# Second layer of a two-layer MLP in fp32 on one core: seven half-size products, before by rounds of four, after as four column streams

## Chip, cores and metric

The kernel runs on one core of a Trainium2 chip. The metric is the device time in microseconds (us) of that core. Three runs of the kernel before gave 2251.70, 2251.74 and 2251.78 us; the median is 2251.74 us.

## What is computed

The input x has 8 sequences of 4096 tokens with 192 channels. A causal convolution with 7 taps (weights by a softmax over the taps, one set for each of 8 heads) gives y. Then comes an MLP on the 32768 tokens with 2048 hidden channels:

```
h = y @ w_in                              # 192 -> 2048
g = h * clip(h + 3.0, 0.0, 6.0) / 6.0
out = g @ w_out                           # 2048 -> 192
```

## The kernel before

The tokens are worked in 32 blocks of 1024 (NB = 32, TB = 1024). A block is two groups of N = 512 tokens. Block 0 goes another way (out_direct) and is not touched, apart from the work that is put beside it. Each of the blocks 1 to 31 runs first_layer (L477) and then second_layer (L532). The loop over the blocks stands at the end of the kernel, and `tc.manual_schedule()` means that every engine's instructions run in the order in which the code emits them.

**First layer.** The weights and y are each split into three parts (HIGH, LOW, MIX) and multiplied with f32r matmuls (L490): 16 steps of 18 matmuls of 512 columns, two at a time on the two halves of the rows. One group of tokens lies on the low partitions and the other on the high ones, so each part of y is also needed with its halves exchanged (`swap`, two DMAs on SP's queue, L265 and L266). ACT scales the partial sums (L501) and makes the clipped factor (relu, L301); DVE multiplies (gate, L305). Between the steps DVE does the convolution of the block after next, one tap at a time (L729). The result g has four quarters A11, A12, A21, A22 (token half by hidden half), each 128 partitions by 8 chunks by 512 tokens.

**Second layer.** The product of the 2 by 2 quarters of g with the 2 by 2 quarters of w_out is done by Strassen's scheme in Winograd's form: seven products instead of eight, with sums S1 to S4 of quarters of g and T1 to T4 of quarters of w_out (table `prod`, L405). S1 = A21 + A22 is added into A21 by a DMA that accumulates, issued by POOL (L528), and S3 = A11 - A21 is made on POOL (g_sums, L401), pair of chunks by pair, at the end of the first layer. S2 = S1 - A11 (into A11) and S4 = A12 - S2 (into A12) are made on DVE by the same helper, four chunks at a time.

A product has 96 output rows, which are three column strips of 32 (q = 0, 1, 2), and 8 chunks of 128 to contract. One matmul (L340) fills one strip of 32 columns of TensorE, so four run at once, in four strips (`tile_position`, `side_by_side` L347). The trace shows each fp32 matmul as two records, which are called passes here. Before, the 7 x 3 x 8 = 168 matmuls of a block go in rounds of four: `three` and `four` pack three strips of one product with one strip of another, and `by_quarters` splits the one strip left over by chunks. That makes 42 rounds, or 84 passes of four. The products are copied (L437, L540) or added (L445) from PSUM into SBUF tiles c0 to c4, transposed (L451) and stored (L359) by ACT, DVE and SP.

Around it stand `high_of` on ACT (L463), the LOW part (L742) and the MIX part (L466) on DVE, and their six exchanging DMAs, all emitted between the first and the second layer by halves_of_y; and conv[0], ACT's first tap (L727), inside the second layer. `left` is the end of a block, which runs inside the next block's first layer.

Of the kernel before, what the change touches and what calls it, by code (L numbers as in the profile page):

```python
# [25 lines left out]
def kernel(  # L26
# [90 lines left out]
    w_out = cst.tile([P, NP, 7, DH], F32, name="w_out")  # L117
    B11, B12, B21, B22, T1, T2, T4 = range(7)
    T3 = B12

    w_in_bits = moe_w_in.bitcast(U32).rearrange("(p s) (c f w) -> c p s f w", s=K3, f=P, w=2)
    w_out_bits = moe_w_out.bitcast(U32).rearrange("(k c p) w -> p c k w", p=P, k=2)
# [268 lines left out]
    def g_sums(engine, which, slots, width):  # L391

        forms = {
            3: (S3, A11, A21, ALU.subtract),
            2: (S2, S1, A11, ALU.subtract), 4: (S4, A12, S2, ALU.subtract),
        }
        for n in which:
            o, a, b, op = forms[n]
            for p in slots[::width]:
                r = slice(p, p + width)  # L400
                engine.tensor_tensor(out=o[:, r], in0=a[:, r], in1=b[:, r], op=op)  # L401


    prod = {
        1: (A11, B11), 2: (A12, B21), 3: (S4, B22), 4: (A22, T4),  # L405
        5: (S1, T1), 6: (S2, T2), 7: (None, T3),
    }

# [11 lines left out]
    def three(n, n4, q4):  # L420
        return four(*[(n, q) for q in range(NQ)], (n4, q4))
# [14 lines left out]
    def piece(dst, q, src, j):  # L436
        nc.scalar.copy(out=dst[rows(q)], in_=src[rows(j)])  # L437
# [21 lines left out]
    def r32(ap):  # L459
        return ap.bitcast(F32R)  # L460
# [13 lines left out]
        nc.scalar.mul(r32(mix), mix, -4096.0)  # L474

    free_slots = list(range(4))

    def first_layer(i, jobs):

        slots = {}  # L480

        def both(n):
            return psum[:, 2 * slots[n] : 2 * slots[n] + 2]

        def mms(n, part, start=False, stop=False):
            group, c = divmod(n, NP)
            for s in range(K3):
                for k in range(2):
                    r = slice(k * D2, (k + 1) * D2)
                    nc.tensor.matmul(  # L490
                        out=psum[:, 2 * slots[n] + k], lhsT=r32(w_in_parts[part][r, c, s]),
                        rhs=r32(y_parts[part][r, group, s]),
                        start=start and s == 0, stop=stop and s == K3 - 1,
                        skip_group_check=True,
                    )

        def begin(n):
            slots[n] = free_slots.pop(0)
            mms(n, HIGH, start=True)
            mms(n, LOW)  # L500
            nc.scalar.mul(both(n), both(n), 4097.0)  # L501

        def end(n):
            group, c = divmod(n, NP)
            mms(n, MIX, stop=True)
            to = g4[:, c, 1:3] if group else g4[:, c, 0::3]
            relu(to, both(n))
            gate(to, both(n))
            free_slots.append(slots[n])

        count = 2 * NP
        begin(0)
        begin(1)
        for job in jobs.get(-1, ()):
            job()
        for n in range(count):
            if n == count - 3:
                begin(n + 2)
            end(n)
            if n < count - 3:  # L520
                begin(n + 2)
            for job in jobs.get(n, ()):
                job()
            if n > NP and n % 2:
                pair = slice(n - NP - 1, n - NP + 1)
                g_sums(nc.gpsimd, (3,), range(NP)[pair], 2)
                if n + 1 < count:
                    nc.gpsimd.dma_start(out=S1[:, pair], in_=A22[:, pair], accum_op=ALU.add)  # L528
                else:
                    add(S1[:, pair], A21[:, pair], A22[:, pair])  # L530

    def second_layer(i, between):  # L532
        last = i + 1 == NB
        ours = [free_slots.pop(0) for _ in range(3 + last)]
        free_banks[:] = [2 * n + k for n in ours for k in range(2)]
        both = nc.sync, nc.scalar
        p1, p2, p4, u2, u3 = (cs.tile([DH, N], F32, name=f"c{k}") for k in range(5))
        two, third = rows_of(0, 2), rows_of(2, 3)
        b, bank = three(1, 2, 0)
        nc.scalar.copy(out=p1[:], in_=bank[m])  # L540
        piece(p2, 0, bank, NQ)
        b, bank = four((2, 1), (2, 2), (4, 0), (4, 1))
        for dst, q, j in ((p2, 1, 0), (p2, 2, 1), (p4, 0, 2), (p4, 1, 3)):
            piece(dst, q, bank, j)
        g_sums(nc.vector, (2,), every, 4)
        add(p2[:], p1[:], p2[:])
        store(i, p2, 0, 0)
        p5 = cs.tile([DH, N], F32, name="c1")
        b7, bank7 = three(7, 4, 2)
        piece(p4, 2, bank7, NQ)  # L550
        g_sums(nc.vector, (4,), every, 4)
        b, bank = three(6, 5, 0)
        piece(p5, 0, bank, NQ)
        add(u2[:], p1[:], bank[m])
        add(u3[:], u2[:], bank7[m])
        add(p4[:], u3[:], p4[:], ALU.subtract)
        store(i, p4, 1, 0)
        for job in between:
            job()
        b, bank = by_quarters(5, 1)  # L560
        pieces(p5, 1, bank)
        add(u2[two], u2[two], p5[two])
        add(p5[two], u3[two], p5[two])
        store(i, p5, 1, 1, range(2))

        def finish(bank, **part):
            t = part.get("tokens", slice(0, N))
            add(u2[:, t], u2[:, t], bank[m, t])
            add(u2[third, t], u2[third, t], bank[rows(NQ), t])
            store(i, u2, 0, 1, **part)  # L570
            add(u3[third, t], u3[third, t], bank[rows(NQ), t])
            store(i, u3, 1, 1, range(2, 3), **part)

        if last:
            for t in range(0, N, N // 2):
                bank = psum[:, take()]
                ts = slice(t, t + N // 2)
                side_by_side(*[
                    product(bank, j, n, q, tokens=ts)
                    for j, (n, q) in enumerate([(3, 0), (3, 1), (3, 2), (5, 2)])  # L580
                ])
                finish(bank, queues=both, tokens=ts)
            return []
        b, bank = three(3, 5, 2)
        free_slots.extend(ours)
        return [lambda: finish(bank)]

    def rows_of(q0, q1):
        return slice(q0 * QS, q1 * QS)
# [18 lines left out]
    with tc.manual_schedule():  # L608
# [106 lines left out]
        while n < len(units):  # L715
# [1 line left out]
            clamp(n + 1)  # L717
            split(n + 2)
            n += 1
        w_sums(((T1, B12, B11), (T2, B22, T1), (T4, T2, B21)))  # L720
        start_pools.close()
        late = ctx.enter_context(tc.tile_pool(name="late", bufs=1, reuse_waits="tile"))
        w_in_parts = [late.tile([P, NP, K3, P], F32, name=f"w_in{n}") for n in range(3)]
# [8 lines left out]
                ))  # L732
            return jobs

        y_parts = []

        def y_high():
            high_of(y_parts[HIGH][:, 0], y[:])
            swap(y_parts[HIGH][:, 1], y_parts[HIGH][:, 0])

        def y_low():
            nc.vector.tensor_tensor(  # L742
                out=r32(y_parts[LOW][:, 0]), in0=y[:], in1=y_parts[HIGH][:, 0], op=ALU.subtract
            )
            swap(y_parts[LOW][:, 1], y_parts[LOW][:, 0])

        def y_mix():
            from_high(y_parts[MIX][:, 0], y_parts[HIGH][:, 0], 1.0 + EPS, y[:], ALU.subtract)
            swap(y_parts[MIX][:, 1], y_parts[MIX][:, 0])

        def halves_of_y():
            y_high()
            y_low()
            y_mix()

        def prepare():
            for n in range(0, NP, 4):
                r = slice(n, n + 4)
                w_parts(*[w[:, r] for w in w_in_parts], w_in[:, r])
            for job in conv_jobs(1):  # L760
                job()
            first_in.close()
            later = ctx.enter_context(tc.tile_pool(name="later", bufs=1, reuse_waits="tile"))
            y_parts.extend(later.tile([P, 2, K3, N], F32, name=f"y{n}") for n in range(3))
            halves_of_y()
            x_tiles[2] = load_x(2, nc.gpsimd)

        out_direct(0, [prepare])
        w_sums(((T3, B22, B12),))
        last = ctx.enter_context(tc.tile_pool(name="last", bufs=1, reuse_waits="tile"))  # L770
        S3 = last.tile([P, NP, N], F32, name="s3")[:]
        cs = ctx.enter_context(tc.tile_pool(name="cs", bufs=1, reuse_waits="tile"))
# [2 lines left out]
        for i in range(1, NB):  # L775
            jobs = {2 * n + 1: [job] for n, job in enumerate(conv[1:])}
            jobs[-1] = left
            if i == 1:
                jobs = {n + 2: job for n, job in jobs.items()}
                jobs[1] = conv[:1]  # L780
            first_layer(i, jobs)
            if i + 1 < NB:
                halves_of_y()
            if i + 2 < NB:
                x_tiles[i + 2] = load_x(i + 2)
            conv = conv_jobs(i + 2) if i + 2 < NB else []
            left = second_layer(i, conv[:1])


# [31 lines left out]
```

## Time and profile before

| | |
|---|---|
| median of three runs | 2251.74 us |
| profiled execution: its time | 2253.59 us |
| its span, first to last instruction | 2251.7 us |
| PE busy | 2242.8 us, 100% of the span |
| DVE busy | 1755.1 us, 78% |
| ACT busy | 1313.6 us, 58% |
| POOL busy | 493.9 us, 22% |
| granted TensorE clock, mean | 0.999 |
| one first layer on the chain | 32.98 us (288 matmuls) |
| one second layer on the chain | 36.19 us (336 passes) |

The profile page gives each engine's busy time, the chain of work that ended last, and the groups of instructions by line with their count, busy time and mean duration. "Idle before" is the time for which the engine did nothing ahead of such instructions, and the arrow names what ended most of it. PE is TensorE, PEld its weight loads, DVE is VectorE, ACT ScalarE, POOL GpSimd, SP SyncE. The timeline answers give the start, the duration and the count of merged instructions.

### The profile page before, as it was taken

What the parts mean: (1) busy time and instruction counts of PE and PEld (TensorE: products, weight loads), DVE (VectorE), ACT (ScalarE), POOL (GpSimd) and SP (SyncE); (2) the same over time, 40 slices, a digit from 0 to 9 for tenths busy, and PEclk for the clock granted to TensorE, in tenths of its full rate; (3) what the DMA queues carried; (4) which work ended last, traced back from release to release, by engine and by line L of the source; (5) the groups of instructions that cost most, each with busy time, mean ns of one, the idle gap of its engine ahead of it and who ended that gap; (6) DMA issues with size and microseconds to landing.
All of it is one profiled execution on the core that took longest, in us unless ns stands there. A gap on an engine that the chain in (4) does not pass through costs nothing.

```text
span 2251.7 us, 46078 instructions
## 1 busy us (share of the span) xinstructions
PE 2242.8 (100%) x20008; PEld 1213.1 (54%) x20008; DVE 1755.1 (78%) x1575; ACT 1313.6 (58%) x1428; POOL 493.9 (22%) x247
## 2 busy tenths in 40 slices
PE   9999999999999999999999999999999999999998
PEld 5445554455544555544555445555455554455544
DVE  8788787778877787877878777887778787787865
ACT  7456654466644666545666446664456654466643
POOL 2322201222112222022221122210222202222112
PEclk9999999999999999999999999999999999999999
DMA  6344335443345443354423554334544335443342
GB/s 155 71 93 90 53 64 99 96 92 63 58 90 99 89 82 53 75 99 92 95 53 59 99 99 89 66 57 87 99 91 85 54 69 99 95 94 56 61 79 43
DMA packets 262442, 182.55 MB, mean 81 GB/s; under 512 B 208992, under 2 KB 214112, under 8 KB 262240
## 3 DMA queue, kind: packets, MB, share of 16 engines
q1 hardware_dynamic: 235928, 129.59, 28.9%
q0 software_dynamic: 25616, 49.82, 12.7%
q8 instruction: 156, 2.56, 0.5%
q14 instruction: 46, 0.38, 0.1%
q10 hardware_dynamic: 696, 0.20, 0.0%
HBM read 31.72 MB, written 25.17 MB: 25 GB/s over the span
## 4 chain that ended last, share of the span: by engine, by line
PE 98%; DVE 1%; ACT 0%; DMA 0%; issue 0%; SPq 0%; ACTq 0%; DVEq 0%
PE psum L340 51%; PE psum L490 45%; PE psum L295 2%; DVE c L445 0%; DMA x<-in_x_dram 0%; DVE xt L451 0%; DVE y L729 0%; DMA out_dram<-xt 0%; ACT y L727 0%; ACT g L301 0%; SPq L100 0%; SPq L132 0%; DVE g L305 0%; DVE top L174 0%; PE psum L623 0%
## 5 line engine op out<-in xcount | busy, mean ns | idle before, releaser
L340 PE MATMUL psum<-g,w_out 128*32 128x512 f32 (+1 forms) x9376 | 1165.4, 590 | 0.0
L490 PE MATMUL psum<-y,w_in 64*128 64x512 f32 x8928 | 1025.1, 388 | 0.5 <-ACT psum L501 0.4
L490 PEld LDWEIGHTS psum<-y,w_in 64*128 64x128 f32 x8928 | 830.0, 184 | 207.9 <-issue 26.0
L401 POOL TENSOR_TENSOR s<-g 128x1024 f32<-128x1024 f32 x124 | 377.4, 3043 | 1624.1 <-DVE g L305 1623.2
L305 DVE SCALAR_TENSOR_TENSOR g<-g,psum 128x1024 f32<-128x1024 f32 (+1 forms) x528 | 618.6, 1186 | 129.8 <-ACT g L301 129.4
L340 PEld LDWEIGHTS psum<-g,w_out 128*32 128x32 f32 x9376 | 340.5, 110 | 650.4 <-issue 638.5
L501 ACT ACTIVATE psum<-psum 128x1024 f32<-128x1024 f32 x496 | 500.3, 1009 | 259.6 <-PE psum L490 257.6
L301 ACT ACTIVATE g<-psum,half 128x1024 f32<-128x1024 f32 (+1 forms) x528 | 565.0, 1088 | 0.8
L437 ACT COPY c<-psum 32x512 f32<-32x512 f32 x248 | 143.4, 578 | 516.4 <-PE psum L340 513.9
L729 DVE SCALAR_TENSOR_TENSOR y<-x,c_sb,y 128x1536 f32<-128x1536 f32 x186 | 337.0, 1812 | 0.2
L445 DVE TENSOR_TENSOR c<-c,psum 96x512 f32<-96x512 f32 (+2 forms) x251 | 170.7, 680 | 211.5 <-ACT c L437 183.2
L401 DVE TENSOR_TENSOR g<-g 128x2048 f32<-128x2048 f32 x124 | 276.8, 2272 | 0.0
L340 PE MATMUL psum<-s,w_out 128*32 128x512 f32 x1488 | 218.3, 592 | 0.0
L340 PEld LDWEIGHTS psum<-s,w_out 128*32 128x32 f32 x1488 | 61.2, 110 | 148.3 <-issue 148.3
L445 DVE TENSOR_TENSOR g<-g 128x1024 f32<-128x1024 f32 x31 | 38.0, 1226 | 130.7 <-POOL s L401 130.7
L528 POOL DMA_DIRECT2D g<-g x93 | 111.7, 1201 | 29.5 <-POOL s L401 29.5
L451 DVE STREAM_TRANSPOSE xt<-c 96x512 f32<-96x512 f32 (+4 forms) x157 | 109.7, 699 | 5.4
L445 DVE TENSOR_TENSOR c<-c,c 96x512 f32<-96x512 f32 (+1 forms) x124 | 84.8, 684 | 5.1 <-ACT c L437 1.9
L540 ACT COPY c<-psum 96x512 f32<-96x512 f32 x31 | 18.0, 581 | 115.7 <-PE psum L340 115.7
L742 DVE TENSOR_TENSOR y<-y,y 128x1536 fp32r<-128x1536 f32 x31 | 54.3, 1752 | 1.6 <-ACT y L463 1.6
L466 DVE SCALAR_TENSOR_TENSOR y<-y,y 128x1536 fp32r<-128x1536 f32 x31 | 54.3, 1752 | 0.0
L463 ACT ACTIVATE y<-y 128x1536 fp32r<-128x1536 f32 x31 | 46.6, 1503 | 12.4 <-DVE y L729 12.4
(53 smaller groups left out, 275.8 us busy)
## 6 DMA issues: line engine op xcount, KB each, us to landing
y<-y SPq DMA_DIRECT2D x186, 384.0 KB, 5.1
g<-g POOLq DMA_DIRECT2D x93, 512.0 KB, 5.3
out_dram<-xt SPq DMA_DIRECT2D x380, 64.0 KB, 2.0
x<-in_x_dram SPq DMA_DIRECT2D x53, 388.5 KB, 7.5
stage<-in_moe_w_in_dram SPq DMA_DIRECT2D x16, 192.0 KB, 4.6
stage<-in_moe_w_out_dram SPq DMA_DIRECT2D x8, 384.0 KB, 5.0
x<-in_x_dram SPq DMA_DIRECT2D x7, 384.0 KB, 7.4
x<-in_x_dram POOLq DMA_DIRECT2D x2, 388.5 KB, 5.5
```

Of the source, the lines that this page charges most:

```text
L301: nc.scalar.activation(r6, h, ACT.Relu, bias=half[:], scale=1.0 / 6.0)
L305: nc.vector.scalar_tensor_tensor(out=g_, in0=g_, scalar=1.0, in1=h, op0=ALU.min, op1=ALU.mult)
L340: lambda p=p: nc.tensor.matmul(out=bank[j * QS : (j + 1) * QS, tokens], lhsT=w_out[:, p, w, cols], rhs=x[:, p, tokens], start=(first and p ...
L401: engine.tensor_tensor(out=o[:, r], in0=a[:, r], in1=b[:, r], op=op)
L437: nc.scalar.copy(out=dst[rows(q)], in_=src[rows(j)])
L445: nc.vector.tensor_tensor(out=out, in0=x, in1=y, op=op)
L451: nc.vector.transpose(out=xt[r, tokens], in_=c[r, tokens])
L466: nc.vector.scalar_tensor_tensor(out=r32(out), in0=high, scalar=scale, in1=x, op0=ALU.mult, op1=op)
L490: nc.tensor.matmul(out=psum[:, 2 * slots[n] + k], lhsT=r32(w_in_parts[part][r, c, s]), rhs=r32(y_parts[part][r, group, s]), start=start an ...
L501: nc.scalar.mul(both(n), both(n), 4097.0)
L528: nc.gpsimd.dma_start(out=S1[:, pair], in_=A22[:, pair], accum_op=ALU.add)
L729: jobs.append(lambda k=k: nc.vector.scalar_tensor_tensor(out=y[:], in0=x[:, :, k : k + N], scalar=c_sb[:, k : k + 1], in1=y[:], op0=ALU.mu ...
```

## The change

In each block two strips of product 7 and two of product 5 (q = 0, 1) are no longer multiplied plainly: those 64 rows are one 2 by 2 product of their own (token halves of 256 by chunk parity; strips q = 0 and 1), and Strassen's scheme is used once more on it: seven small products, each of 4 matmuls of 256 columns and 32 rows. Their sums are made by `small_sums`: for product 7 into a tile s7 (three on POOL, the third on DVE), for product 5 into A22 (four on POOL, once product 4 has read A22). The small weights are made once by `small_weights`.

The matmuls are written as four streams, one for each strip. Streams 0 to 2 hold products 1, 4, 6, 2, 3 with strip q in stream q, and one chunk each of the third strip of product 5: 41 matmuls of 512 columns. Stream 3 holds the rest: 13 matmuls of 512 columns and 56 of 256. A clock in units of one pass of 512 columns (a matmul of 512 columns is 2 units, one of 256 is 1) orders the matmuls of all streams and the work of the other engines (`put`, `do`). Each stream ends at 82 units. Several results are added in PSUM: a bank that ACT copied from another is added onto by the next products.

DVE and not POOL makes S3 for the last two pairs of chunks. S4 goes to S3's place. The LOW and MIX parts of y (split_rest) are made at unit 28 of the second layer, behind the sums on DVE, and the exchanges are issued at unit 48 into a tile that shares its memory with s7.

```diff
@@ first_layer, after step n
-                g_sums(nc.gpsimd, (3,), range(NP)[pair], 2)
+                g_sums(nc.gpsimd if n + 3 < count else nc.vector, (3,), range(NP)[pair], 2)
@@
+    def small_sums(to, x, which, engine=nc.gpsimd):
+        x11, x12, x21, x22 = four_parts(x)
+        s1, s2, s3, s4 = four_parts(to)
+        forms = {
+            1: (s1, x21, x22, ALU.add), 2: (s2, s1, x11, ALU.subtract),
+            3: (s3, x11, x21, ALU.subtract), 4: (s4, x12, s2, ALU.subtract),
+        }
+        for n in which:
+            o, p, q, op = forms[n]
+            engine.tensor_tensor(out=o, in0=p, in1=q, op=op)
@@ second_layer (the old body goes)
+        s7 = pools[0].tile([P, NP, N], F32, name="s7", tag="other")[:]
+        s5 = A22
+        A, V, B, E, C = (bank[rows(3)] for bank in (e, v, f, d, a))
+        def put(j, cost, fn):
+            streams[j].append((clock[j], fn))
+            clock[j] += cost
...
+        for q in range(NQ):
+            plain(q, a, 1, q, every, True)
+            plain(q, d, 4, q, every, True)
+            plain(q, e, 5, 2, range(5 + q, 6 + q), True)
+            plain(q, b, 6, q, every)
+            plain(q, a, 2, q, every)
+            plain(q, b, 3, q, every)
+        def do(t, fn, *args, **kw):
+            streams[3].append((t - 0.5, lambda: fn(*args, **kw)))
+        small_sums(s7, S3, (1, 2, 4))
+        plain(3, v, 7, 2, range(4), True)
+        small(7, 1, A, lo, True, range(2))
+        plain(3, v, 7, 2, range(4, 6))
+        small(7, 1, A, lo, False, range(2, 4))
+        do(clock[3], copy, out=B[:, lo], in_=A[:, lo])
+        plain(3, v, 7, 2, range(6, NP))
+        do(clock[3], copy, out=p7[third], in_=V)
+        small(7, 2, A, lo)
+        do(clock[3], copy, out=p7[first, lo], in_=A[:, lo])
+        plain(3, v, 5, 2, range(0, 2), True)
+        small(7, 6, B, lo)
+        do(clock[3], copy, out=C[:, lo], in_=B[:, lo])
+        small(7, 5, E, lo, True)
+        do(clock[3], copy, out=p7[second, lo], in_=E[:, lo])
+        small(7, 7, C, lo)
+        do(clock[3], add, p7[second, hi], C[:, lo], p7[second, lo])
+        small(7, 3, B, lo)
+        do(clock[3], add, p7[second, lo], B[:, lo], p7[second, lo])
+        small(7, 4, C, lo)
+        do(clock[3], copy, out=p7[first, hi], in_=C[:, lo])
...
+        do(16, copy, out=b[m], in_=a[m])
+        do(16, g_sums, nc.vector, (2,), every, 4)
+        do(16, small_sums, s7, S3, (3,), nc.vector)
+        do(32, small_sums, s5, S1, (1, 2, 3, 4))
+        do(34, copy, out=p5[third], in_=e[first])
+        do(34, add, p5[third], p5[third], e[second])
+        do(34, add, p5[third], p5[third], e[third])
+        for t, job in zip((28, 56), between):
+            do(t, job)
+        if not last:
+            do(48, swap_parts)
+        do(50, add, u3[:], b[m], p7[:])
+        do(50, add, o[:], u3[:], d[m])
+        do(50, store, i, o, 1, 0)
+        do(50, g_sums, nc.vector, (4,), every, 4)
+        do(66, store, i, a, 0, 0)
...
+        events = sorted(((t, fn) for st in streams for t, fn in st), key=lambda x: x[0])
+        for _, fn in events:
+            fn()
@@ the loop over the blocks
             if i + 1 < NB:
-                halves_of_y()
+                high_of(y_own[HIGH][:], y[:])
...
-            left = second_layer(i, conv[:1])
+            left = second_layer(i, [split_rest, *conv[:1]] if i + 1 < NB else [])
```

In the part cut out, stream 3 goes on in the same way with product 5 (small products 1, 5, 2, 6, 7, 3, 4, with the plain chunks 2 to 4 of its third strip between them), from unit 48 to 82.

## The prediction

> **What bounds the kernel now.** First the chain that ended last, on the page and in the stretch of one block, then the groups by line.
>
> ```profile
> PE 98%; DVE 1%; ACT 0%; DMA 0%; issue 0%; SPq 0%; ACTq 0%; DVEq 0%
> ```
> ```profile
> 1000.10 32.98 PE psum L490 x288
> 1033.08 36.19 PE psum L340 x336
> ```
>
> The chain is TensorE from end to end, and a block is 32.98 + 36.19 = 69.17 us. So passes taken out of the second layer shorten the span, and every wait that TensorE has to sit out lengthens it. 36.19 us for 84 passes of four is 0.4308 each; with the change of layer taken off I use 0.4297 us, one unit of the change's clock.
>
> ```profile
> L401 POOL TENSOR_TENSOR s<-g 128x1024 f32<-128x1024 f32 x124 | 377.4, 3043 | 1624.1 <-DVE g L305 1623.2
> L401 DVE TENSOR_TENSOR g<-g 128x2048 f32<-128x2048 f32 x124 | 276.8, 2272 | 0.0
> ```
> ```profile
> L340 PE MATMUL psum<-g,w_out 128*32 128x256 f32 x128 | 7.1, 379 | 0.0
> L742 DVE TENSOR_TENSOR y<-y,y 128x1536 fp32r<-128x1536 f32 x31 | 54.3, 1752 | 1.6 <-ACT y L463 1.6
> L466 DVE SCALAR_TENSOR_TENSOR y<-y,y 128x1536 fp32r<-128x1536 f32 x31 | 54.3, 1752 | 0.0
> L466 DVE SCALAR_TENSOR_TENSOR w_in<-w_in,w_in 128x1536 fp32r<-128x1536 f32 x4 | 12.3, 3138 | 0.3 <-ACT w_in L463 0.3
> ```
>
> The two L466 groups decide this case. Same instruction, same shape, two inputs in SBUF: 1752 ns in the blocks, 3138 ns in the mean where w_in is split. The timeline of that place, DVE then POOL, shows the company it has there; the last line is POOL's instruction by itself:
>
> ```profile
> 66.28 9.00 DVE L466 SCALAR_TENSOR_TENSOR w_in<-w_in,w_in 128x1536 fp32r<-128x1536 f32 x3 [0.33 <-ACT w_in L463]
> 67.12 9.87 POOL L211 TENSOR_TENSOR w_out<-w_out 128x768 f32<-128x768 f32 x3
> ```
> ```profile
> 99.11 1.83 POOL L211 TENSOR_TENSOR w_out<-w_out 128x768 f32<-128x768 f32 x1 [7.56 <-PE psum L340]
> ```
>
> Three of POOL's take 9.87 us, 3.29 each, where one alone takes 1.83; and 1.75 + 1.83 = 3.58. So DVE and POOL don't work at once here: they take turns, one instruction each, and a turn that begins on the other's end is about 0.13 us shorter than the instruction alone. Before, no second layer shows this: DVE's sums and POOL's stand apart.
>
> **The change, part by part.** 0 is the first matmul of the second layer.
>
> *TensorE.* Streams 0 to 2 have 82 units, 82 x 0.4297 = 35.24 us. The half matmul: 128 records in fours are 32 passes in 7.1 us, 0.222, or 0.216 without the last one's drain. So stream 3 takes 26 x 0.4297 + 112 x 0.2158 = 35.34 us. Against 84 x 0.4297 = 36.10 the gain is 0.75 us a block, if nothing waits.
>
> *S3 on DVE.* The last three gates stand in the timeline like this:
>
> ```profile
> 1033.10 3.48 DVE L305 SCALAR_TENSOR_TENSOR g<-g,psum 128x1024 f32<-128x1024 f32 x3 [1.34 <-ACT g L301]
> ```
>
> 1033.10 is my 0. Between them comes a sum of 1024 elements (1.23, row of L445) after the first gate, then one after the last, then the sum S1: 3.6 + 3 x 1.23 + gaps = 7.4. S3 is whole at 6.2. Its last chunk is read at unit 15, 6.4: no wait. Before, DVE waited 4.2 us for POOL here (130.7 us over 31 blocks), so the step itself gains DVE time.
>
> *The sums of 7 and 5 on POOL.* Each has 1024 elements in strides. The row 128x1024 has a mean of 3.04, with waits for DVE in it; the timeline has 2.40 for one undisturbed. The strided form isn't in the trace; between 2.27 (a turn) and 3.04 I take the row it is nearest to, 2.40. All seven read SBUF.
>
> *DVE beside them.* From 7.4 on its queue holds, in this order: S2 in two halves (2.25 each), the third sum of s7 (1.23), LOW and MIX of y (1.75 each), two additions into p5 from PSUM (0.69 each), then the addition that reads bank C. The first five have two inputs in SBUF. Whether a TENSOR_TENSOR of DVE waits as the SCALAR_TENSOR_TENSOR does, no row shows. Its bounds are no wait and a whole turn of POOL's. I take the turn, by the nearest row, L466: an elementwise instruction of DVE with two SBUF inputs too.
>
> The Trainium skill, page "SBUF — State Buffer", section "Who interferes with whom", says that a DVE instruction with two SBUF inputs contends with a GpSimd instruction that reads SBUF, and that the port pair is an exclusive lock. By it the sum is the one I make; by rows of one opcode alone it would be rival 2.
>
> So the turns are, with 0.13 off each: POOL s1 2.27 to 9.7; DVE S2 2.12 to 11.8; POOL s2 to 14.1; S2 2.12 to 16.2; POOL s4 to 18.5; DVE s3 1.10 to 19.6; POOL (first sum of 5; product 4 has read A22 by unit 32) to 21.8; LOW 1.62 to 23.45; POOL to 25.7; MIX to 27.35; two additions of PSUM 1.4, no turn, to 28.75; the addition from C 0.43 to 29.2.
>
> *What TensorE waits for.* Its queue is in order, so a stream that waits stops all four. Small product 6 of 7 wants s2 at unit 28, 12.0; it has it at 14.1: **2.1 late**. Small product 7 wants s3 at unit 36, 15.5 + 2.1 = 17.6; 19.6: **2.0 late**. Small product 4 adds onto C, which DVE must have read, at unit 44, 18.9 + 4.1 = 23.0; 29.2: **6.2 late**. After that nothing is: s5's last two sums end by 32, S4 has POOL's quiet, and 4 units (1.7 us) cover each of ACT's copies (32x512 takes 0.58; 256 wide and into PSUM isn't shown, from 0.3 to 0.58, and 1.7 hides either) and DVE's 0.43. Sum 10.3.
>
> *The rest.* Six exchanges are issued at unit 48 and read 34 units and 8 first-layer steps later, 14.6 + 16 us: hidden, and the stores behind them on SP are waited for by none. LOW and MIX are wanted at 35: there at 27.35, but without stalls too at 17. conv[0] is still one ACT instruction in the second layer. ACT's first layer (1.01 + 1.11 for a step, no idle) gets nothing new. The eight small_weights (nearest row: 384 wide, 1.0; at most 8 us) have the 33 us of a first layer as cover. The tail: before 4.1 us from the last pass to the last store's issue; after, a copy 0.6 and three halves of 0.42 + 0.44: same within 0.5.
>
> *The clock.* A gap of 6.2 us may cost more than itself.
>
> ```profile
> 2245.20:2249.00 3.80, 0.00 (x0) 0.00 (x0) 3.54 (x9) 0.00 (x0) 0.00 (x0) 1.00 0.46 70
> 2249.20:2251.70 2.50, 0.00 (x0) 0.00 (x0) 0.00 (x0) 0.00 (x0) 0.00 (x0) 0.50 0.27 42
> ```
> ```profile
> L631 PE MATMUL psum<-zeros 128*128 128x512 f32 x6 | 5.3, 1058 | 1.5 <-DVE half L232 1.5
> ```
>
> The third column from the end is the granted clock: full for 4.1 us after the last matmul (2245.0), then half. At the start the first 6 matmuls (L631, 1058 ns against 592) take 5.3 us at half speed. So after a gap of 6.2 a block can run 5 us at half speed and lose 2.5. Bounds 0 and 2.5; the gaps of 2 are under 4.1. I take 2.5 in four blocks of five, 2.0, since 6.2 is half as much again as the one gap measured.
>
> The page "TensorE: Matmul & The Clock Gate", section "HAM oscillation — how this bites in real kernels", names idle gaps over about 3.4 us, by a free-running window; by that figure too 6.2 is too long in most blocks, and my sum would stay.
>
> **Sum.** A block with y to split: 10.3 - 0.75 = 9.55, and 2.0 of clock. Thirty such blocks: 346.5 us. The last block has no LOW and MIX, so its C is read in time: 4.1 - 0.75 = 3.4. Together +350 us on the span of 2251.7; the profiled execution took 2253.59 with it, 1.85 more than the median of 2251.74. What lies around the span stays, so the median goes to **2602 us**.
>
> **Rivals.**
> 1. *No turns* (ends faster). DVE's sums and POOL's run at once, as they would if the turns at 66 us came of something that the second layer hasn't got. Then DVE reads C at 18.5 with 18.9 to spare, no wait is left, and 31 x 0.75 = 23 us are gained: **2228 us**. It decides from turns of DVE shorter than 0.4 us in all. For it: no TENSOR_TENSOR of DVE is seen waiting. Against: L466, three turns in a row. 0.12.
> 2. *Only SCALAR_TENSOR_TENSOR takes turns.* MIX alone waits, C is read 1.0 late, the gain of 0.75 is spent: +0.3 a block, **2260 us**. 0.04.
> 3. *Turns, but the clock holds.* 2251.7 + 30 x 9.55 + 3.4: **2542 us**. 0.18.
> 4. *The change doesn't do what it says*: short passes beside long ones don't fit two in one, or banks are waited for that I count free. If all 112 took 0.43, stream 3 would be 24 us longer a block: **3000 us**. The row 0.216 is against it. 0.04 with all else above 2690.
>
> The forecast has 0.62. The range holds it and rival 3: the low end is turns without the two of product 5 (4.5 less) and no clock, 30 x 5.0 + 3.4 = 153, so 2405, and 25 us for a strided sum that is quicker, 2380; the high end is no shortening of turns (1.2 a block) and 2.5 of clock, 2251.7 + 30 x 13.2 + 3.4 = 2651, and 40 for unseen waits: 2690. Left out: 0.12 + 0.04 + 0.04. Measurement tells 0.2% from no change; faster by more 0.12, within 0.02 (rival 2 with a little luck), slower 0.86.
>
> **What would show it.** After: DVE's L401 sums and the L466 row far above 2272 and 1752 ns, POOL's small sums far above 2.4; weight loads of TensorE with idle time ended by POOL s7, by DVE s7 and by DVE's addition from C, 2, 2 and 6 us; the clock under 1.0 in the second half of a second layer. Wrong if DVE's rows stay as they are: then rival 1.

## The result and the profile after

The changed kernel takes 2605.9 us (median; 2605.0 to 2606.6), the kernel before 2251.7 beside it: 1.157 times as long, 95% interval 1.156 to 1.159. The forecast was 2602.

The span is 2603.5 us. The chain that ended last was TensorE for 98% before; now the page has:

```profile
PE 35%; issue 27%; DVE 16%; POOL 15%; DMA 5%; ACT 1%; SPq 0%; DVEq 0%; POOLq 0%; ACTq 0%
```

These shares can't be read as what bounds the kernel. TensorE is busy for 90% of the span. Of 712 us of "issue", 575 are 14 stretches of 40 to 42 us in which the chain goes back along POOL's queue through POOL's idle time (one runs from 1055.69 to 1095.92); TensorE is busy all through this one. The stretch of one block, below, is the safer reading.

The groups show what the sums cost now (count, busy us, mean ns). First the page, then the answer that keeps shapes apart:

```profile
L556 POOL TENSOR_TENSOR g<-g 128x1024 f32<-128x1024 f32 x124 | 407.1, 3304 | 2.4
L556 POOL TENSOR_TENSOR s<-s,s 128x1024 f32<-128x1024 f32 x62 | 266.2, 4293 | 4.9
L402 DVE TENSOR_TENSOR g<-g 128x2048 f32<-128x2048 f32 x62 | 238.3, 3880 | 33.1 <-DMA g<-g 33.1
```
```profile
L862 DVE TENSOR_TENSOR y<-y,y 128x1536 fp32r<-128x1536 f32 x31 | 119.5, 3855 | 1.6 <-ACT y L464 1.6
L467 DVE SCALAR_TENSOR_TENSOR y<-y,y 128x1536 fp32r<-128x1536 f32 x31 | 118.4, 3819 | 0.0
L556 DVE TENSOR_TENSOR s<-s 128x1024 f32<-128x1024 f32 x31 | 105.0, 3387 | 0.0
```

The S2 halves (L402) take 3.88 us and not 2.27, LOW (L862) 3.86 and not 1.75, MIX (L467) 3.82 and not 1.75, the third sum of s7 on DVE 3.39 where 1024 elements take 1.23. The small sums on POOL take 3.3 to 4.3 where one with nobody beside it takes 2.36. A record here takes in the wait for the turn: the second half of S2 in the block below has one of 4.44 us, from 1115.74 to 1120.18, for 2.27 us of work. So both engines look busy for longer than they work.

The list of waits, with total us, times and the longest, shows who waits for them:

```profile
PEld psum L588 <- DVE c L446: 189.8, 30, 6.3
PE psum L588 <- DVE c L446: 174.2, 30, 5.8
...
PEld psum L588 <- POOL s L556: 58.1, 31, 2.1
PE psum L588 <- DVE s L556: 58.1, 31, 1.9
...
DVE g L402 <- DMA g<-g: 33.1, 28, 2.2
...
PE psum L588 <- POOL s L556: 30.0, 31, 1.2
```

Three waits in each block: for s2 of product 7 from POOL (31 times, 1.9), for s3 from DVE (31 times, 1.9), and for the addition that reads C (L446, 30 times, 5.8). The last block has no LOW and MIX, hence 30. A wait can show twice, once for the weight load (PEld) and once for the matmul; it counts once.

The chain of one block (start, us, what), whose second layer begins at 1104.06:

```profile
1104.25 9.06 DMA g<-g
...
1113.43 2.21 DVE g L402
1115.64 0.08 issue
1115.73 0.05 DVEq L556
1115.78 0.10 DVE g L402
1115.87 4.23 issue
1120.11 3.39 DVE s L556
1123.49 3.85 DVE y L862
1127.35 3.81 DVE y L467
...
1132.62 0.44 DVE c L446
1133.06 0.04 issue
1133.11 19.00 PE psum L588 x88
```

TensorE is not on it until 1133.11, 29.05 us into the layer; DVE's queue is. "issue" of 4.23 is the second half of S2: no event of the profile says that DVE waits for POOL's turn, so the page has no releaser to name. Such pieces, of 4.1 to 4.3 us, are only 34 of the 712 us of issue on the page.

The same block by stretches (after the engines' columns: granted clock, DMA share, GB/s):

```profile
1118.00:1131.00 13.00, 7.33 (x80) 3.70 (x80) 13.00 (x4) 1.28 (x3) 12.84 (x5) 1.00 0.20 46
1131.00:1133.10 2.10, 0.00 (x0) 0.00 (x0) 1.95 (x4) 0.00 (x0) 2.10 (x1) 0.55 1.00 243
1133.10:1140.00 6.90, 6.89 (x49) 3.48 (x53) 3.20 (x5) 1.16 (x3) 2.58 (x2) 0.64 0.85 185
1140.00:1152.00 12.00, 12.00 (x134) 7.07 (x125) 5.94 (x6) 2.13 (x4) 0.00 (x0) 1.00 0.22 34
```

The clock falls to half inside the wait for C and stays there for 6.83 us (in 24 of the 30 blocks) or 3.41 us (in 6).

### The profile page after: what moved, and what is told of

It reads as the page before. It is cut to its first block, busy times and chain, and to the rows that moved or that the text cites. A ratio compares the mean times of both kernels' runs of the same rounds, so it can differ in the third digit from the quotient of the medians.

```text
span 2603.5 us, 49775 instructions
## 1 busy us (share of the span) xinstructions
PE 2331.1 (90%) x21432; PEld 1456.9 (56%) x21432; DVE 2096.0 (81%) x1605; ACT 1317.2 (51%) x1552; POOL 1120.9 (43%) x410
## 3 DMA queue, kind: packets, MB, share of 16 engines
q8 instruction: 168, 2.75, 0.4%
## 4 chain that ended last, share of the span: by engine, by line
PE 35%; issue 27%; DVE 16%; POOL 15%; DMA 5%; ACT 1%; SPq 0%; DVEq 0%; POOLq 0%; ACTq 0%
PE psum L498 19%; PE psum L588 13%; POOL g L556 7%; DMA g<-g 4%; POOL s L556 4%; POOL s L402 4%; DVE g L402 3%; DVE g L306 3%; DVE y L862 2%; DVE y L467 2%; DVE s L556 2%; PE psum L296 2%; DVE s L402 2%; PE psum L341 2%; DVE c L446 1%
## 5 line engine op out<-in xcount | busy, mean ns | idle before, releaser
L402 POOL TENSOR_TENSOR s<-g 128x1024 f32<-128x1024 f32 x62 | 210.7, 3399 | 1254.1 <-DVE g L306 1254.1
L588 PE MATMUL psum<-s,w_out 128*32 128x512 f32 (+1 forms) x2728 | 602.5, 534 | 0.0
L498 PE MATMUL psum<-y,w_in 64*128 64x512 f32 x4464 | 522.6, 389 | 0.6 <-ACT psum L509 0.4
L498 PE MATMUL psum<-y_other,w_in 64*128 64x512 f32 x4464 | 517.0, 386 | 1.3 <-DVE g L306 1.3
L588 PE MATMUL psum<-s,w_s 128*32 128x256 f32 x992 | 279.5, 439 | 262.3 <-DVE c L446 174.2
L498 PEld LDWEIGHTS psum<-y,w_in 64*128 64x128 f32 x4464 | 413.5, 184 | 104.6 <-issue 13.2
L498 PEld LDWEIGHTS psum<-y_other,w_in 64*128 64x128 f32 x4464 | 415.7, 184 | 92.2 <-ACT psum L509 5.1
L556 POOL TENSOR_TENSOR g<-g 128x1024 f32<-128x1024 f32 x124 | 407.1, 3304 | 2.4
L556 POOL TENSOR_TENSOR s<-s,s 128x1024 f32<-128x1024 f32 x62 | 266.2, 4293 | 4.9
L402 DVE TENSOR_TENSOR g<-g 128x2048 f32<-128x2048 f32 x62 | 238.3, 3880 | 33.1 <-DMA g<-g 33.1
L446 DVE TENSOR_TENSOR c<-psum,c 32x256 f32<-32x256 f32 (+1 forms) x187 | 95.6, 511 | 186.2 <-ACT c L630 106.5
L588 PE MATMUL psum<-g,w_s 128*32 128x256 f32 x992 | 234.3, 379 | 0.0
```

Source lines behind the costliest of these rows:

```text
L446: nc.vector.tensor_tensor(out=out, in0=x, in1=y, op=op)
L498: nc.tensor.matmul(out=psum[:, 2 * slots[n] + k], lhsT=r32(w_in_parts[part][r, c, s]), rhs=r32(y_other[0][r, part, s] if group else y_own[ ...
L556: engine.tensor_tensor(out=o, in0=p, in1=q, op=op)
L588: nc.tensor.matmul(out=out, lhsT=w, rhs=x, start=start, stop=True, tile_position=(0, j * QS), skip_group_check=True,)
```

## The experiments

Times of each group stand beside runs of the kernel before on the same chip, with medians of 2251.8 to 2253.2 us. e1, e2, e3, e8, e9 and e10 are one run each, e5 and e7 four, e4 and e6 five. Diffs are against the changed kernel unless another one is named. "Second layer" is the mean over the blocks 1 to 30, from its first matmul to the next first layer's: 36.2 us before, 47.8 after the change.

**e1: LOW and MIX later.** The theory: turns of DVE and POOL make the sums late, and three waits follow. If so, what is queued ahead of the addition from C sets the third wait.

```diff
-        for t, job in zip((28, 56), between):
+        for t, job in zip((45, 56), between):
```

> LOW and MIX of y move from unit 28 to unit 45 of the second layer, behind DVE's addition that reads bank C. Theory (DVE and POOL take turns, and two turns stand ahead of that addition): the third wait of TensorE (6.0 us in every block) goes, and with it the half clock; waits of 1 to 2.5 us come later instead (S4, bank a), because the two turns now stand ahead of S4. Second layer about 42.3 us in place of 47.8, span about 2440, mean clock over 0.99. Rival (C is read late because of the copies within PSUM or because of what POOL does, whatever stands ahead of it on DVE): about 2606, the 6.0 us gap stays.

2507.1 us, clock 0.985, 67 above the 2440 expected. The wait for C is gone, but another of 3.6 us has come, 31.2 us into the layer:

```profile
PE psum L588 <- DVE c L446: 90.8, 30, 3.0
```

The trace has it as small product 5 of product 5, which waits for DVE's addition o (`add, o[:], u3[:], d[m]` in the change). They share no data: the product goes into rows 96 to 127 of a bank, o reads rows 0 to 95 of that bank. The expectation had waits for S4 and for bank a, and not this one. e9 tests such a wait, in the order of e4.

**e2: no turns.**

```diff
-            engine.tensor_tensor(out=o, in0=p, in1=q, op=op)
+            if engine is nc.gpsimd:
+                engine.memset(o, 0.0)
+            else:
+                engine.tensor_tensor(out=o, in0=p, in1=q, op=op)
```

> POOL's small sums of s7 and s5 become memsets of the same tiles, which read nothing (the sums are left out, so the small products are of other data); DVE's work and the order are unchanged. Theory: no turns, so DVE's L402, L556 and the rows of LOW and MIX go back to 2.27, 1.23 and 1.75 us, the first two waits go, and the third is at most 1.6 us, what the late landing of the accumulating DMA (9.3 us) leaves of it: 2228 to 2280 us. Rival (DVE's queue is too long for unit 44 by its own order, turns or not): a third wait of 4 us or more, the clock under 1.0, over 2450 us.

2257.5 us, clock 0.999. With nobody who reads SBUF on POOL, DVE's rows are those of before:

```profile
L402 DVE TENSOR_TENSOR g<-g 128x2048 f32<-128x2048 f32 x62 | 141.9, 2292 | 43.2 <-DMA g<-g 40.5 <-PE psum L591 2.5
```

POOL has less to do here too (a memset takes 0.95 to 1.44 us for 2.36), but in the block that starts at 1036 us LOW runs beside two memsets and takes 1.76 us. The turns are nearly all of the 350 us. The end of the row tells what is late next: S2 waits for the accumulating DMA that makes S1. It landed 9.06 us after its issue in the block shown above (median 7.5 after the change). That is why the time is not under that of before.

**e3: product 5's sums left out.**

```diff
-        do(32, small_sums, s5, S1, (1, 2, 3, 4))
```

> The four small sums of product 5 on POOL are left out (its small products read A22 as it is). Theory: LOW and MIX then have no turns to wait for, C is read two turns (4.5 us) sooner, the third wait falls from 6.0 to about 1.5, the first two stay at 2.0 and 2.1, and no gap is long enough for the half clock: 30 x 5.0 + 3 over before, about 2405 us. Rival (the third wait comes from s7's sums or from PSUM): the 6 us gap stays, about 2600.

2408.1 us, clock 1.0, second layer 41.2. The count of turns gives the size of the wait: without product 5's sums on POOL the third gap between passes is 1.90 us in the place of 6.2, and with no gap above 2.3 us the clock stays at 1.0.

**e4: another order of the same work.**

```diff
-        do(16, g_sums, nc.vector, (2,), every, 4)
         do(16, small_sums, s7, S3, (3,), nc.vector)
+        do(16, g_sums, nc.vector, (2,), every, 4)
...
-        do(34, add, p5[third], p5[third], e[second])
-        do(34, add, p5[third], p5[third], e[third])
-        for t, job in zip((28, 56), between):
+        do(44, add, p5[third], p5[third], e[second])
+        do(44, add, p5[third], p5[third], e[third])
+        for t, job in zip((72, 76, 80), between):
...
-            do(48, swap_parts)
+            do(78, swap_parts)
+        do(50, g_sums, nc.vector, (4,), range(4), 4)
         do(50, add, u3[:], b[m], p7[:])
         do(50, add, o[:], u3[:], d[m])
         do(50, store, i, o, 1, 0)
-        do(50, g_sums, nc.vector, (4,), every, 4)
+        do(50, g_sums, nc.vector, (4,), range(4, NP), 4)
```

S3's third pair, chunks 4 and 5, goes back to POOL too (the expectation of e6 calls it the seventh), and LOW, MIX and ACT's first tap are the three jobs between.

> Same work in another order, made from the turns: S3 of chunks 4 and 5 on POOL again, the third sum of s7 ahead of S2 on DVE, the two additions into p5 at unit 44, the first half of S4 ahead of u3, LOW, MIX and the exchanges at units 72, 76 and 78, conv[0] at 80. Theory, by adding up turns: s2 by 11.8, s3 by 9.5, C read at 18.7, one wait of 0.2 for S2, no gap: second layer 35.6 us, 31 x 0.5 us under before, about 2236. Rival (waits come from elsewhere too, or late LOW and MIX hold up the next first layer by 1 us or more): 2260 to 2300.

2343.8 us, ratio 1.0405 (1.039 to 1.042): a miss by 108. All three waits for sums are gone; one gap of 2.75 us is left, and its chain is this:

```profile
948.81 0.70 DVE s L402
949.51 3.11 issue
952.62 0.70 DVE c L446
953.32 0.02 issue
953.34 0.70 DVE c L446
954.04 0.14 issue
954.17 12.24 PE psum L588 x64
```

S4's first half (L402, with a turn in it), then u3, then o, then TensorE: again small product 5 of product 5 and the bank of o.

**e5: the clock alone.** Eighteen matmuls that nobody reads, in the other three strips, fill the wait for C.

```diff
+        def keep_busy():
+            for c in range(6):
+                for j in range(NQ):
+                    matmul(j, v[rows(j)], w_out[:, c, B21, j * QS : (j + 1) * QS], A12[:, c], c == 0)
+        do(clock[3] + 0.4, keep_busy)
```

> Tests the clock term by itself. Eighteen extra matmuls of 512 columns (six in each of the three strips that stream 3 does not use, into a bank whose other rows are free, read by nobody) are put just ahead of the small product that waits 6.2 us for C. Order, sums and waits of DVE and POOL stay as in the changed kernel, so the wait itself stays. Theory: the half clock comes from that one gap (in the changed kernel the granted clock falls to half for 3.41 or 6.83 us after it and nowhere else); with work in the gap the clock stays at 1.0 and each second layer loses its 2.4 us: 2606 - 30 x 2.4 = 2534 us, between 2525 and 2550. Rival: the half clock hits only passes that wait anyway, so it costs nothing and the time stays at 2606; or the extra passes are themselves on the path and it rises.

2543.9 us, ratio 1.129 (1.127 to 1.131), against 1.157 without them: 2.2 us less in each second layer (45.58 for 47.80), given back in part by the last block, which had no such wait to fill (4.5 us more from its second layer to the end). The two stretches of one second layer, before and after the place of the wait, are at full clock:

```profile
888.41:917.50 29.09, 29.09 (x257) 23.97 (x258) 25.86 (x22) 27.26 (x28) 3.94 (x2) 1.00 0.10 15
917.50:933.90 16.40, 16.40 (x162) 7.69 (x158) 13.12 (x10) 8.83 (x11) 12.37 (x6) 1.00 0.78 145
```

So more work made it 62 us faster, and the rival that the half clock costs nothing falls.

**e6: a third order.** Against e4, with the waits for banks counted:

```diff
-        do(50, g_sums, nc.vector, (4,), range(4), 4)
         do(50, add, u3[:], b[m], p7[:])
         do(50, add, o[:], u3[:], d[m])
-        do(50, store, i, o, 1, 0)
-        do(50, g_sums, nc.vector, (4,), range(4, NP), 4)
+        do(50, g_sums, nc.vector, (4,), range(4), 4)
+        do(62, store, i, o, 1, 0)
         do(66, store, i, a, 0, 0)
+        do(66, g_sums, nc.vector, (4,), range(4, NP), 2)
...
-        do(44, add, p5[third], p5[third], e[second])
-        do(44, add, p5[third], p5[third], e[third])
-        for t, job in zip((72, 76, 80), between):
+        do(41, add, p5[third], p5[third], e[second])
+        do(45, add, p5[third], p5[third], e[third])
+        for t, job in zip((75, 79), between):
```

The exchanges go to 80, and the first tap becomes a tensor_scalar on POOL behind `left`.

> All the work of the changed kernel, in a third order that keeps clear of both kinds of wait seen so far: turns of DVE and POOL, and an engine that reads a PSUM bank while TensorE wants to write other rows of it. On DVE: the small sum S3 ahead of the two halves of S2, the two additions to p5 at once after the additions of product 7, u3 and o ahead of the first half of S4, the second half of S4 in two pieces behind the two reads of a and o, LOW and MIX behind the last small sums; S3's seventh pair on POOL; the first tap of the convolution on POOL at the start of the next first layer in the place of ACT in the second. Theory: by the durations in the trace of the changed kernel every operand is there when its pass is due, but for S2's second half (0.2 to 0.3 us late); the second layer takes 82 x 0.4297 + 0.3 = 35.5 to 36.0 us in the place of 36.19 before, so 2232 to 2250 us with the clock at 1.0, at or a little under the kernel before. Rival 1: some wait by bank or turn is left, as in the other order (a gap of 2.75 us in each layer, 2344); one such wait of 1 us would give 2265. Rival 2: the sums on POOL simply do not fit beside DVE's, whatever their order, and the second layer stays at or above 38 us: 2310 or more.

2239.5 us, ratio 0.994 (0.993 to 0.995); second layer 35.8, with no gap above 0.434 us between passes in the block that starts at 820 us. The sums do fit, and turns are still taken: the S2 halves take 4.47 us each, more than in the changed kernel. They cost nothing where nobody waits. Rivals 1 and 2 of this run fall, but for the lateness of 0.2 to 0.3 us that e7 takes up; it makes no gap that shows in the trace.

**e7: the last lateness.** Against e6:

```diff
-            plain(q, b, 6, q, every)
-            plain(q, a, 2, q, every)
+            plain(q, a, 2, q, every[:1])
+            plain(q, b, 6, q, every)
+            plain(q, a, 2, q, every[1:])
```

Small products 5 and 2 of product 5 change places, and u3, o and S4's first half go from 50 to 52.

> The third order, with what is still late there taken away: the second half of S2 comes at 18.26 us in the trace of the third order, and its first pass is due at 42 units x 0.4297 = 18.05. One pass of the product with A12 is put ahead of the product with S2 in the three full streams, so S2 is due 0.86 us later; so that the small product 5 of product 5, which waits for the addition that reads its bank, is not late then, it changes places with small product 2; u3, o and the first half of S4 come two units later. Theory: the second layer goes from 35.79 to 35.4 to 35.55 us, so 2239.5 - 31 x 0.3 = 2230 us, between 2226 and 2234. Rival: that lateness is not on the path, because the fourth stream sets the end; then 2239.5 stays. A second rival: the later u3 runs into a turn with POOL's last small sums or o makes a small product wait by its bank; then 2245 or more.

2230.1 us, ratio 0.990 (0.989 to 0.992), the fastest of all. The chain of one block has nothing but TensorE again:

```profile
748.96 35.54 PE psum L588 x219
784.50 32.92 PE psum L498 x288
```

**e8: u3 and o first.** One edit against e4: `g_sums(..., (4,), range(4), 4)` behind u3 and o.

> One edit against the other order (2343.8): u3 and o are put ahead of the first half of S4 on DVE again. No matmul, sum or unit changes. Theory: the one gap of 2.75 us in that order is small product 5 of product 5 waiting for o, which reads other rows of the bank that it writes; o then ends at about 23.1 us in the place of 26.6, before that product is due (23.2, or 24 with the 0.8 us by which the stream is late), so the gap goes and 2.3 us of each layer with it: 2343.8 - 31 x 2.3 = 2272 us, between 2262 and 2282. Rival: the gap is the stream waiting for its own operands (S4 or POOL's sums, as in the changed kernel), and then the later S4 leaves the time at 2344 or makes it worse.

2282.8 us, just above the expected range. The gap of 2.75 is gone, as expected; the second layer is 37.1, and 2.3 us less would have been 36.8. What is left are two gaps of 0.6 and 0.54 (0.43 is none) near its end: POOL's third sum of product 5 stood waiting from 22.9 to 28.5, and the fourth came late.

**e9: E in a bank of its own.** One edit against e4:

```diff
-        A, V, B, E, C = (bank[rows(3)] for bank in (e, v, f, d, a))
+        A, V, B, E, C = (bank[rows(3)] for bank in (e, v, f, psum[:, 2 * free_slots[0]], a))
```

> One edit against the other order (2343.8): the fourth stream's region E, into which small product 5 of product 5 is accumulated, is moved from the bank d, whose other rows the addition o reads, to a bank of the fourth slot, which nobody uses during the second layer. Order and data are the same. Theory: the gap of 2.75 us is no wait for data but for the bank: o reads rows 0 to 95 of d and the product writes rows 96 to 127 of it. With a bank of its own the product need not wait and the gap goes: 2343.8 - 31 x 2.3 = 2272 us, between 2262 and 2285. Rival: the product waits for data that comes at the same time as o by chance (POOL's sums); then the gap and 2344 stay.

2257.2 us: the gap is gone without a change of order or data, so the wait was for the bank. The second layer is 36.2, 2.8 less than in e4 (39.06): all of the gap, since S4 stays ahead of u3 and the sums on POOL are in time. The time is below the expected range of 2262 to 2285, which had taken off 2.3 us a layer.

**e10: no transpose between S4's halves.** One edit against e8: `store(i, o, 1, 0)` behind both halves.

> One edit against the order with u3 first (2282.8): the transpose of o stands behind both halves of S4 on DVE and not between them. In that kernel DVE did the first half of S4, the transpose (0.70 us, one input) and the second half (2.25 us, as alone) with POOL's sum waiting through all three, where other places show strict turns. If the transpose in between is what lets DVE keep its turn, POOL's third sum of product 5 now runs between the halves: it ends near 27.9 us of the second layer in the place of 30.7, the fourth near 32.3 in the place of 33.1, the small gaps at 33 and 35 us shrink, and the time falls by up to 0.4 us a layer to about 2270. If turns go by something else, such as who asked first, the trace shows POOL waiting through both halves again, and 2283 stays.

2264.8 us, but not by the reason given. DVE (its timeline: start, us) does both halves on end, 4.48 us for two that take 2.27 each alone:

```profile
853.52 0.68 DVE L446 TENSOR_TENSOR c<-c,psum 96x512 f32<-96x512 f32 x1
854.13 4.48 DVE L402 TENSOR_TENSOR s<-g 128x2048 f32<-128x2048 f32 x2
858.53 0.70 DVE L452 STREAM_TRANSPOSE xt<-c 96x512 f32<-96x512 f32 x1
```

POOL's sum, which began at 853.64, waits through both and takes 7.2 us. So the transpose isn't what lets DVE go twice; the time falls because S4 and what follows end 0.6 us sooner. Which of two that want a turn gets it stays open (below).

## Why the prediction was right

**TensorE.** The gain of 0.75 us a block was nearly right: 82 units in the place of 84. e7, with nothing late, has 35.55 for the 36.19 of before, 0.64. Its 2230 us are what rival 1 called 2228, and it needs another order for that, not the absence of turns.

**The turns.** Right for both opcodes. No row of before showed a TENSOR_TENSOR of DVE waiting; three do now (2.27 to 3.88, 1.75 to 3.86, 1.23 to 3.39). The Trainium skill's page "SBUF — State Buffer", section "Who interferes with whom", draws the line by the number of inputs in SBUF and not by the opcode; these three rows agree with it, and rival 2, which drew it by opcode, falls.

**The three waits.** 2.1 + 2.0 + 6.2 = 10.3 predicted; in the block above stream 3 goes on 1.95, 2.07 and 6.01 us later than its passes before would have let it, 10.03. The order and the ends of the turns came out as listed, within 0.3 us (s2 at 14.0 for 14.1, the addition from C at 29.0 for 29.2).

**The clock.** 2.0 us a block was the term with the thinnest ground, from one gap at the end of the kernel. e5 measures 2.2. Every block but the last has a stretch at half clock; on average 4.6 us of it lie behind the wait, half of which is 2.3. The prediction took the 4.1 us of that one gap as the time for which the clock holds. Here the clock fell 2.5 to 5.8 us after the start of the last pass, and in e1 and e4 it fell after shorter gaps. So the place of the loss was right, and its size in part luck. Rival 3 gave 2542 for a clock that holds; e5 makes it hold and has 2543.9.

**What was costed at nothing.** small_weights was, and rightly: eight instructions of 0.46 us on POOL, done long before its next sum. But the first layer of block 1 is 1.7 us longer, for which the sum had no term. The trace shows TensorE waiting there for DVE, whose last two taps of the convolution (two inputs in SBUF) stand beside POOL's sums of S3 and take 3.0 us in the place of 1.8: a turn again. The last block is 2.6 us longer against 3.4 predicted. So the sum closes: 1.75 + 347.5 for thirty blocks + 2.6 = 351.8 us, the difference of the spans. Of one block, 10.0 of waits + 2.2 of clock - 0.64 is 11.6, as measured (47.80 - 36.19).

**Where it was wrong without harm.** Rival 1's condition was mis-stated: "no wait is left" without turns. e2 takes the turns away and has 2257.5: the accumulating DMA lands late, and S2 with it. The sum had S1 whole at 7.4 us; in the block above the DMA lands at 9.25. In the changed kernel that wait stood behind POOL's first turn, which ended at 9.6, so the forecast didn't feel it, and that was luck. By e2 the rival ends at about 2257, just slower than before, and the chance of 0.12 given to faster had no case under it.

**What was left out.** Waits by PSUM bank stood in rival 4 as something that might be there. None binds in the changed kernel, but they decided e1 and e4, where the expectation missed by 67 and 108 us. The Trainium skill's page "PSUM — Partial Sum Buffer", section "PSUM bank collisions raise a hardware error", says that two engines may use one bank at the same time if their 32-row quadrants differ. No run here tries that: the waits are in the program, by whole bank.

**The change itself.** It isn't the second Strassen step that costs 350 us, but the place of LOW and MIX and of S2 in DVE's queue beside seven sums on POOL. The same matmuls and sums in e7's order, with the first tap and S3's third pair on POOL, are 1% faster than before.

## What to carry over

Before moving sums to an idle POOL, add its SBUF time to that of every DVE instruction with two SBUF inputs in the same stretch: the two are one queue, and what counts is which of its results is due first. Then put the sums that TensorE waits for ahead and the others behind, and, where the program's waits go by whole bank as here, count a PSUM bank as one resource: a read of any of its rows by DVE holds back the next matmul into it. A gap of TensorE near 3 us or more can cost the clock too (here from 2.75 us between passes on, never at 2.3), and filling it with idle matmuls is a quick test of how much.

## What was not expected of the hardware

- **Shorter gaps than thought slow the clock.** A gap of 2.75 us between passes cost 1.7 us in 3 of 30 blocks (e4), one of 3.6 in about 7 of 10 (e1), one of 6.2 in all. The Trainium skill's page "TensorE: Matmul & The Clock Gate", section "HAM oscillation — how this bites in real kernels", names idle gaps over about 3.4 us. The idle time in e1's gap is 3.0 us and in e4's 2.2, both under it, so by these runs the figure is no safe limit.
- **Turns don't always alternate.** In the changed kernel they did, from POOL's first sum of 7 to MIX. In e8 and e10 DVE had two in a row (S4's halves) while POOL's sum waited for 4.8 us and more. There POOL's record begins 0.5 us before that of DVE's first half. What decides was not found.
- **An accumulating DMA of 512 KB** takes 7.5 us from issue to landing in the median, 9.06 in the block shown; before the change the median was 5.3. Why it is later stays open.
- **Short passes ran two in the time of one long one**, beside long ones in the other strips: 0.216 us from one to the next, beside 0.430. In the block of e7 that is shown, streams 0 to 2 and stream 3 end within 0.25 us of each other.
